# A fused attention and token-MLP kernel: one score tile moved from the end to the head of 39 stretches

## The chip, the core and the metric

The kernel runs on one core of a Trainium2 chip. A core has a matrix engine (TensorE, in the profile PE, with its weight loads as PEld), a vector engine (VectorE, DVE), a scalar engine (ScalarE, ACT), a general engine (GpSimd, POOL) and a queue that issues transfers (SyncE, SP). Each works through its own instructions in the written order and waits at semaphores for the others. Matrix products land in PSUM, which has eight banks of 128 x 512 fp32 numbers; VectorE and ScalarE read them from there.

The metric is the device time of one execution in microseconds (us); lower is better. Three runs of the kernel before gave 1671.33, 1671.52 and 1672.03 us, so the median is 1671.52 us.

## The reference

```python
x = A_x                                             # 2048 tokens x 640
g = _sigmoid((x * gate_w).sum(-1, keepdims=True))
a = _A_ref(x, A_wq, A_wk, A_wv, A_wo)               # attention: 32 heads of 20, one shared k and v
b = _B_ref(x, B_w1, B_b1, B_w2, B_b2)               # token MLP: W2 gelu(W1 layernorm(x)), over the tokens
return g * a + (1 - g) * b
```

Inside `_A_ref` the scores are `q @ k.T * 20 ** -0.5`, softmax runs over the 2048 keys, and the result goes through `wo`. Inside `_B_ref` the products are 2048 x 1728 and 1728 x 2048 for 640 channels. All is fp32: each large product is split into a high and a low part and done as three products of a faster type.

## The kernel before, in words

**Attention.** The work is cut into 32 groups (`NU`), each of four heads and 512 queries, and each group into 16 blocks of 128 keys: 512 units. Two kinds of score tiles are made, each of 128 x 512 numbers, one matmul and one PSUM bank:

- a *max tile* (`ms_next`, matmul at L479): queries on the rows. VectorE reduces it to a column of row maxima (`tensor_reduce`, L482). The maxima of a group must be known before its exponentials. There are 64 of them to a group, 2048 in all.
- an *exponent tile* (`s_next` and `qk`, L657): keys on the rows. ScalarE takes its exponential into SBUF (L660). Four belong to a unit.

When a unit is finished, `pv_mm` (L684) multiplies its four exponent tiles with v, in eight matmul records that run over four column parts of the array at a time.

**The banks.** From the start of the long middle part on (`ring`), max tiles and exponent tiles take turns on two pools of three banks each (`next_bank`). So whatever the kind, a tile gets the bank that the sixth tile before it had, and its matmul can start only when that tile has been reduced or exponentiated.

**Two row halves.** A score tile has only 60 or 62 rows of weights and takes one half of the 128 rows of the matrix array. In a stretch, one half (`b`) makes score tiles while the other half (`1 - b`) makes products of the MLP or of the projection, 320 columns wide (L929, L750 or L875, tile `g`). All products of an item, from both halves, add up in the one bank of `ps_g`. As the two halves must not write that bank at the same time, the first product of a stretch waits for a flag that VectorE writes after the last product of the stretch before (`signal`, L670). When an item is complete, its `done` has ScalarE copy the bank out (L758 for the second MLP product, L888 for the projection), and the next item's first product waits for that too.

**Stretches.** The list `ph` holds 326 stretches, and `main(k, vs)` writes out each. Even ones (call them *single*) finish one unit at their end, odd ones (*double*) two. The halves swap roles from stretch to stretch. A stretch has two lanes:

- the score lane, on half `b`: a string of `m` (max tile) and `s` (exponent tile), 11 letters, or 10 in one case;
- the product lane, on half `1 - b`: a string in which `F` is all products of the stretch, then the flag, then `done` if the item ends there, and `m` is a max tile on that half.

`merged` writes them into one order: at each step the lane goes that has used less time, with 0.232 us counted for a score tile and 0.147 us for a product. Two pairs of strings exist, by the number of products (`FEW` up to 15, `MANY` above), each for double and single:

```python
FEW = (("smsssmssmmm", "mFm"), ("smsmsmssms", "Fm"))
MANY = (("msmsmsssmsm", "Fm"), ("msmsmsssmsm", "Fm"))
```

**Which stretches there are.** 0 to 119: the first MLP product (20 items of six stretches, 16 products each). 120 to 249: the second MLP product for 13 blocks of tokens (26 items of five stretches with 16, 17, 16, 16 and 16 products). 250 to 285: the same for the last three blocks (six items of six stretches with 13 or 14 products). 286 to 325: the projection of ten blocks (20 items of two stretches with 15 products). After these follow `BLOCKS`, where no max tiles are left.

Between the lanes' work and the units, `main` also lets short pieces of older work go (`settle`: the transposes L700 and L712 and the reciprocal L705 that finish a group, on VectorE, at the end of double stretches), and reduces and stores row maxima (L493, L503).

Of the kernel before, what the change touches and what calls it, by code (L numbers as in the profile page):

```python
# [39 lines left out]
def mix_kernel(ctx: ExitStack, tc: tile.TileContext, A_x, A_wq, A_wk, A_wv, A_wo,  # L40
# [426 lines left out]
    def ms_next(b):  # L467
        k = given[b]
        if k >= 32 * NU:
            return None  # L470
        given[b] += 1
        n, r = divmod(k, 32)
        (kq, pr), qt = divmod(r // 4, 2), r % 4

        def step():
            if n not in mtiles:
                mtiles[n] = mpool.tile([P, 16, 4], F32, name="mp")
            ms = next_bank()
            nc.tensor.matmul(ms, qmax[n][64 * b:64 * b + 60, pr, qt * P:(qt + 1) * P],  # L479
                             kst[64 * b:64 * b + 60, kq * NB:(kq + 1) * NB], start=True, stop=True)  # L480
            c = (2 * b + pr) * 4 + qt
            nc.vector.tensor_reduce(mtiles[n][:, c, kq:kq + 1], ms, axis=AX.X, op=ALU.max)  # L482
            issued[b] += 1
            if min(issued) == 32 * n + 1:
                new_qmax(n + 1)

        return step

    def ms_done():
        n = len(row_max)  # L490
        if n < NU and min(issued) >= 32 * (n + 1):
            mm = mmpool.tile([P, 16], F32, name="mm")
            nc.vector.tensor_reduce(mm, mtiles.pop(n), axis=AX.X, op=ALU.max)  # L493
            mn = mmpool.tile([P, 2, 16], F32R, name="mn")
            nc.gpsimd.tensor_scalar(mm, mm, -1.0, None, op0=ALU.mult)
            nc.gpsimd.tensor_copy(mn[:, 0, :], mm)
            nc.gpsimd.tensor_sub(mn[:, 1, :], mm, f32(mn[:, 0, :]))
            row_max[n] = mn

    def store_max(n):  # L500
        mn = row_max[n]
        mt = mpool.tile([P, 32], F32, name="mt")
        nc.vector.transpose(mt, f32(mn).rearrange("p j c -> p (j c)"))  # L503
        nc.sync.dma_start(out=m_scr[n], in_=mt)

    def fetch_max(n):
        src = m_scr[n].rearrange("(i j b r) e -> j b r i e", j=2, b=2, r=8)
        for b in range(2):
            for j in range(2):
                rows = f32(qtiles[n][64 * b + 60 + j:64 * b + 61 + j])  # L510
                nc.sync.dma_start(out=rows.rearrange("o p (t i e) -> o (p t) i e", i=4, e=32), in_=src[j, b][None])
# [131 lines left out]
    def s_next(b):  # L643
        j = sc[b]
        if j >= 2 * len(units):
            return None
        sc[b] += 1
        return lambda: qk(j // 2, j % 2, b)
# [202 lines left out]
    def tail_take(h, n):  # L851
        out = []
        while len(out) < n and tail[h] and tail[h][0][0] in loaded:
            out.append(tail[h].pop(0)[1])
        return out
# [101 lines left out]
    def stretches(seq):  # L957
        return [(rows[1 - b], rest if b else [], done if b else []) for rows, rest, done in seq for b in range(2)]

    ph = stretches(seq)  # L960
    ph[0][1].append(lambda: twin_u(0))
    m = len(ph)
# [27 lines left out]
    def merged(lx, lf):  # L990
        lanes, at, out = (list(lx), list(lf)), [0.0, 0.0], []
        while lanes[0] or lanes[1]:
            k = 0 if lanes[0] and (not lanes[1] or at[0] <= at[1]) else 1
            us, f = lanes[k].pop(0)
            if f:
                out.append(f)
            at[k] += us
        return out
# [5 lines left out]
    def settle(wide=False):  # L1004
        for _ in range(2 if spare[0] else 1):
            if later and (wide or spare[0] or not later[0][0]):
                f = later.pop(0)[1]
                if f:
                    f()
        pop_chain()  # L1010
# [6 lines left out]
    def main(k, vs):  # L1017
        b = k % 2
        fs, rest, done = ph[k]
        fill = [(F_US, f) for f in fs] + [(0.0, f) for f in [signal] + done]  # L1020
        if not vs:
            lx = [(3 * X_US, ms_next(b)), (3 * X_US, ms_next(b)), (X_US, s_next(b)), (X_US, ms_next(b))]
            lx += [(X_US, s_next(b)) for _ in range(3)]
            lf = fill + [(X_US, s_next(1 - b))]
        else:
            sx, sf = (MANY if len(fs) > 15 else FEW)[len(vs) == 1]
            lx = [(X_US, (s_next if c == "s" else ms_next)(b)) for c in sx]
            lf = []
            for c in sf:
                lf += fill if c == "F" else [(X_US, (s_next if c == "s" else ms_next)(1 - b))]  # L1030
        order = merged(lx, lf)
        known, kept = set(row_max), set(sent)
        wide = len(vs) == 2
        parted = wide and units[vs[0]][1] == NS - 1
        for i, f in enumerate(order):
            if wide and i == (len(order) + 1) // 2:
                settle()
                if parted:
                    pv_mm(vs[0])
            f()  # L1040
        ms_done()
        spare[0] = len(row_max) == NU
        settle(wide and not parted)
        if vs:
            n, kb = units[vs[0]][0] + 1, units[vs[0]][1]
            if n in kept and n not in back_in:
                fetch_max(n)
                back_in.add(n)
        for f in rest:
            f()  # L1050
        if vs and kb > 4 and n in known and n not in sent and n < NU:
            store_max(n)
            sent.add(n)
        for v in vs[parted:]:
            pv_mm(v)
# [3 lines left out]
    for k in range(len(ph)):  # L1059
        n = 0 if k == 0 else 1 + k % 2  # L1060
        main(k, list(range(v, v + n)))
        v += n
        if k == len(ph) - 4:
            raw = last_wo()
        if k == len(ph) - 2:
            w_last = split_last(raw)
# [5 lines left out]
    for n in BLOCKS:  # L1072
# [4 lines left out]
        while any(sc[b] < ends[b] for b in range(2)):  # L1077
# [4 lines left out]
        fs = [tail_take(b, len(tail[b]) if n == left else  # L1082
                        max(0, round(((own[b] + len(tail[b]) * F_US) * n / left - len(lanes[b]) * X_US) / F_US)))
              for b in range(2)]
# [79 lines left out]
```

## Time and profile before

| | |
|---|---|
| median of three runs | 1671.52 us |
| the profiled execution's own time | 1671.47 us |
| its span | 1669.7 us |
| TensorE busy | 1661.0 us (99%) |
| VectorE busy | 1435.7 us (86%) |
| ScalarE busy | 1188.0 us (71%) |
| GpSimd busy | 606.3 us (36%) |
| max tiles reduced (L482) | 1514 + 534 |
| exponent tiles (L660) | 1512 + 536 |

The span is 1.8 us shorter than the profiled execution's time; that execution lies 0.05 us under the median. The granted clock of TensorE is 1.00 over the whole span. A matmul counts as busy from its issue to its modelled end, and matmuls of the two row halves overlap, so 99% says that TensorE nearly always had one under way, not that it ran at its peak. In the rows of a timeline, the first number is the start in us from the span's start, the second the time that the row covers; `x3` merges three instructions of one kind. Tile names `ms` and `s` are the two bank pools, not the two kinds of tile: the kind is told by the line, L479 for a max tile and L657 for an exponent tile.

### The profile page before, as it was taken

What the parts mean: (1) busy time and instruction counts of PE and PEld (TensorE: products, weight loads), DVE (VectorE), ACT (ScalarE), POOL (GpSimd) and SP (SyncE); (2) the same over time, 40 slices, a digit from 0 to 9 for tenths busy, and PEclk for the clock granted to TensorE, in tenths of its full rate; (3) what the DMA queues carried; (4) which work ended last, traced back from release to release, by engine and by line L of the source; (5) the groups of instructions that cost most, each with busy time, mean ns of one, the idle gap of its engine ahead of it and who ended that gap; (6) DMA issues with size and microseconds to landing.
All of it is one profiled execution on the core that took longest, in us unless ns stands there. A gap on an engine that the chain in (4) does not pass through costs nothing.

```text
span 1669.7 us, 38827 instructions
## 1 busy us (share of the span) xinstructions
PE 1661.0 (99%) x14865; PEld 1105.5 (66%) x14865; DVE 1435.7 (86%) x2732; ACT 1188.0 (71%) x2346; POOL 606.3 (36%) x759
## 2 busy tenths in 40 slices
PE   9999999999999999999999999999999999999998
PEld 7899666666666666666666666666666566666665
DVE  6689899999989999988888988988888998988933
ACT  4434777777777777777777777777777777777775
POOL 6578555455455554422232332122122220111210
PEclk9999999999999999999999999999999999999999
DMA  7665222222132232222222222212222121333611
GB/s 211 205 176 137 79 71 69 78 58 78 53 84 73 71 82 74 58 60 62 66 75 74 55 62 66 61 52 71 63 66 60 55 65 41 96 111 113 189 51 39
DMA packets 178305, 138.20 MB, mean 83 GB/s; under 512 B 33306, under 2 KB 144055, under 8 KB 178119
## 3 DMA queue, kind: packets, MB, share of 16 engines
q1 hardware_dynamic: 177830, 135.39, 28.9%
q8 instruction: 117, 1.92, 0.5%
q14 instruction: 70, 0.57, 0.1%
q10 hardware_dynamic: 288, 0.33, 0.1%
HBM read 102.36 MB, written 31.65 MB: 80 GB/s over the span
## 4 chain that ended last, share of the span: by engine, by line
PE 95%; issue 2%; DVE 1%; SPq 1%; ACT 0%; DMA 0%; POOL 0%; POOLq 0%; DVEq 0%; ACTq 0%
PE o L684 28%; PE ms L479 18%; PE s L657 13%; PE g L750 10%; PE g L929 7%; PE ms L657 5%; PE pp L298 4%; PE s L479 3%; PE pu L586 3%; PE g L875 2%; DVE mp L482 1%; PE ms L831 0%; ACT p L660 0%; PE pt L290 0%; SPq L195 0%
## 5 line engine op out<-in xcount | busy, mean ns | idle before, releaser
L482 DVE TENSOR_REDUCE mp<-ms 128x1 f32<-128x512 f32 x1514 | 967.2, 685 | 130.2 <-PE ms L479 102.7
L660 ACT ACTIVATE p<-s 128x512 f32<-128x512 f32 x1512 | 820.6, 606 | 299.4 <-PE s L657 280.2
L479 PE MATMUL ms<-kst,qmx 60*128 60x512 f32 x1514 | 646.5, 433 | 1.7 <-DVE mp L482 1.7
L657 PE MATMUL s<-qst,kst 62*128 62x512 f32 x1512 | 601.6, 403 | 0.0
L684 PE MATMUL o<-p,v_sb 128*32 128x512 f32 x4096 | 511.3, 601 | 0.0
L479 PEld LDWEIGHTS ms<-kst,qmx 60*128 60x128 f32 x1514 | 279.0, 184 | 244.9 <-ACT p L660 114.7
L482 DVE TENSOR_REDUCE mp<-s 128x1 f32<-128x512 f32 x534 | 355.6, 683 | 12.0 <-PE s L479 11.8
L660 ACT ACTIVATE p<-ms 128x512 f32<-128x512 f32 x536 | 305.1, 599 | 56.8 <-PE ms L657 50.2
L657 PEld LDWEIGHTS s<-qst,kst 62*128 62x128 f32 x1512 | 278.5, 186 | 55.2 <-DVE flag L670 31.0
L929 PE MATMUL g<-slot,wh 64*128 64x320 f32 x1280 | 297.5, 311 | 0.0
L129 POOL TENSOR_TENSOR wl<-wr,wh 128x512 fp32r<-128x512 f32 x176 | 228.6, 1300 | 43.8 <-PE g L750 17.3
L479 PE MATMUL s<-kst,qmx 60*128 60x512 f32 x534 | 230.8, 441 | 0.4 <-DVE yo L525 0.4
L684 PEld LDWEIGHTS o<-p,v_sb 128*32 128x32 f32 x4096 | 97.5, 108 | 185.3 <-issue 177.2
L657 PE MATMUL ms<-qst,kst 62*128 62x512 f32 x536 | 216.8, 405 | 0.0
L929 PEld LDWEIGHTS g<-slot,wh 64*128 64x128 f32 x1280 | 211.6, 184 | 2.0 <-issue 1.7
L750 PE MATMUL g<-slot,wh 64*128 64x320 f32 x864 | 202.1, 313 | 0.1
L750 PE MATMUL g<-u,wh 64*128 64x320 f32 x864 | 201.7, 312 | 0.0
L929 PE MATMUL g<-slot,wl 64*128 64x320 f32 x640 | 199.6, 312 | 0.0
L706 POOL TENSOR_TENSOR ot<-ot,rl 128x512 f32<-128x512 f32 x30 | 31.6, 1052 | 346.6 <-DVE rl L705 346.6
L128 POOL CAST wh<-wr 128x512 fp32r<-128x512 f32 x144 | 88.3, 613 | 188.0 <-PE g L750 81.5
L750 PEld LDWEIGHTS g<-slot,wh 64*128 64x128 f32 x864 | 143.5, 184 | 4.9 <-ACT yo L758 4.0
L750 PEld LDWEIGHTS g<-u,wh 64*128 64x128 f32 x864 | 143.5, 184 | 1.1 <-issue 1.1
(202 smaller groups left out, 2092.8 us busy)
## 6 DMA issues: line engine op xcount, KB each, us to landing
wr<-in_B_w_dram SPq DMA_DIRECT2D x152, 256.0 KB
qmx<-q_scr SPq DMA_DIRECT2D x192, 80.0 KB
qst<-q_scr SPq DMA_DIRECT2D x192, 80.0 KB
slot<-o_scr SPq DMA_DIRECT2D x20, 320.0 KB
y_scr<-yo SPq DMA_DIRECT2D x16, 320.0 KB
o_scr<-oh SPq DMA_DIRECT2D x124, 40.0 KB
o_scr<-ol SPq DMA_DIRECT2D x124, 40.0 KB
q_scr<-qh SPq DMA_DIRECT2D x19, 256.0 KB
```

Of the source, the lines that this page charges most:

```text
L128: nc.gpsimd.tensor_copy(wh, wr)
L129: nc.gpsimd.tensor_sub(wl, wr, f32(wh))
L298: nc.tensor.matmul(pp, w, t, start=first and n == 0, stop=not more and n == len(steps) - 1)
L479: nc.tensor.matmul(ms, qmax[n][64 * b:64 * b + 60, pr, qt * P:(qt + 1) * P], kst[64 * b:64 * b + 60, kq * NB:(kq + 1) * NB], start=True, s ...
L482: nc.vector.tensor_reduce(mtiles[n][:, c, kq:kq + 1], ms, axis=AX.X, op=ALU.max)
L586: nc.tensor.matmul(pu[r][:, :HD2], w[rows, c, :], h[rows, st, :], start=(st == 0 and k == 0), stop=(st == NS - 1 and k == 2))
L657: nc.tensor.matmul(s, kst[64 * b:64 * b + 62, kb * P:(kb + 1) * P], q[64 * b:64 * b + 62, pr, :], start=True, stop=True)
L660: nc.scalar.activation(p, s, AF.Exp, scale=SCALE)
L684: nc.tensor.matmul(o[32 * hh:32 * hh + 32, :], v_sb[:, kb, :], ptiles.pop((u, hh)), start=(kb == 0), stop=(kb == NS - 1), skip_group_check ...
L750: other_tile(half, nc.tensor.matmul(hold["p"][:, :HD2], w[r, fc % HS, :], u[d][r, fc, :], start=(hold["n"] == 1), stop=(hold["n"] == 6 * F ...
L875: other_tile(half, nc.tensor.matmul(hold["p"][:, :HD2], o[r, c, :], w[r, c, d * HD2:(d + 1) * HD2], start=(hold["n"] == 1), stop=(hold["n" ...
L929: other_tile(half, nc.tensor.matmul(hold["p"][:, :HD2], w[r, st % HS, :], h[d][r, st, :], start=(hold["n"] == 1), stop=(hold["n"] == 6 * NS)))
```

## The change

A condition is added after the strings are chosen. It holds where the stretch before ended an item (`ph[k - 1][2]`) and where either a double stretch has more than 15 products or a single one has at most 15. Then one `m` of the product lane's string goes to its head: `Fm` becomes `mF`.

```diff
             sx, sf = (MANY if len(fs) > 15 else FEW)[len(vs) == 1]
+            if k and ph[k - 1][2] and (len(vs) == 2) == (len(fs) > 15):
+                sf = "m" + sf.replace("m", "") + "m" * (sf.count("m") - 1)
             lx = [(X_US, (s_next if c == "s" else ms_next)(b)) for c in sx]
```

It holds for 39 stretches: 13 double ones with 16 products (125, 135, ... 245), six single ones with 13 (250, 256, ... 280), and 20 single ones with 15 (286, 288, ... 324). The first MLP product has none: behind its items come single stretches with 16 products. No instruction is added or taken away. In these stretches the order becomes, with `X` for a tile of the score lane by number and kind, `M` for the moved max tile, and `F` for a product:

```
16 products, double   before  X0m F F X1s F X2m F F X3s ... X9s F X10m flag M
                      after   X0m M X1s F F X2m F F X3s ... X9s F F X10m F flag
15 products, single   before  X0s F F X1m F F X2s F X3m ... F F X9s flag M
                      after   X0s M X1m F F X2s F F X3m ... F X9s F F flag
```

## The prediction

> **What bounds the kernel now.** I read the page first (busy shares, the chain that ended last), then who waited for ScalarE's copies of finished items, then timelines of single stretches, engine by engine.
>
> ```profile
> span 1669.7 us, 38827 instructions
> ...
> PE 1661.0 (99%) x14865; PEld 1105.5 (66%) x14865; DVE 1435.7 (86%) x2732; ACT 1188.0 (71%) x2346; POOL 606.3 (36%) x759
> ...
> PE 95%; issue 2%; DVE 1%; SPq 1%; ACT 0%; DMA 0%; POOL 0%; POOLq 0%; DVEq 0%; ACTq 0%
> ```
>
> TensorE's stream sets the end: the chain lies on it for 95%. So each stretch is worth what moves its first matmul on v (L684, behind which the next stretch begins). VectorE's 86% is the other number to watch.
>
> ```profile
> L758 ACT ACTIVATE yo<-g,b2g,og_half x32: 633/643/654, 710.6 to 1416.5; 128x320 f32<-128x320 f32 x32
> ...
>   PEld g L750: 4.0, 13
> ```
>
> Products waited 13 times for the copy of a finished item. Those are the 13 double stretches that the change touches. The first of them (stretch 125), TensorE, then ScalarE, then VectorE:
>
> ```profile
> 710.80 0.50 PE L479 MATMUL ms<-kst,qmx 60*128 60x512 f32 x1
> 711.27 0.41 PE L750 MATMUL g<-slot,wh 64*128 64x320 f32 x1
> 711.28 0.50 PE L657 MATMUL s<-qst,kst 62*128 62x512 f32 x1
> ...
> 711.62 0.39 PE L479 MATMUL ms<-kst,qmx 60*128 60x512 f32 x1
> ...
> 713.51 0.50 PE L479 MATMUL ms<-kst,qmx 60*128 60x512 f32 x1
> 713.57 0.30 PE L750 MATMUL g<-slot,wh 64*128 64x320 f32 x1
> 713.72 0.40 PE L479 MATMUL s<-kst,qmx 60*128 60x512 f32 x1
> 714.05 0.64 PE L684 MATMUL o<-p,v_sb 128*32 128x512 f32 x4
> ...
> 710.58 0.64 ACT L758 ACTIVATE yo<-g,b2g,og_half 128x320 f32<-128x320 f32 x1
> ...
> 711.33 3.46 DVE L482 TENSOR_REDUCE mp<-ms 128x1 f32<-128x512 f32 x5
> 714.72 0.69 DVE L482 TENSOR_REDUCE mp<-s 128x1 f32<-128x512 f32 x1
> ```
>
> X0 starts at 710.80. The first product waits until the copy ends (710.58 + 0.64 = 711.22) and starts at 711.27; X1, behind it in the queue, at 711.28. From X2 (711.62) to X10 (713.51) a score tile follows each (713.51 - 711.62)/8 = 0.236 us, of which I use 0.23. The 16 products take 2.30 us from first to last: 0.25 for the first step, then (2.30 - 0.25)/14 = 0.146 each. M starts at 713.72, the v matmuls at 714.05: 3.25 us from X0. There is a real wait to fill: the first product starts 0.47 us behind X0.
>
> **What the change does to banks.** Nothing is added; M, a max tile, goes from the end to behind X0. A tile takes the bank of the sixth tile before it, so the order decides who waits for whom. With M at the head, in a 16-product stretch X6 takes M's bank, X8 that of X2 and X10 that of X4: all reduced by VectorE, in the order X0, M, X2, X4. Before, X10 had X4's bank too, but VectorE had no M ahead of it. In a single stretch of 10 score tiles X6 now takes M's bank, X7 that of X1, X9 that of X3, behind reductions M, X1, X3.
>
> The profile already has a stretch with that head, unchanged by the edit: the double one with 15 products, X0 M X1 (`mFm`). Its X7, the ninth tile, takes the bank of X1, the third.
>
> ```profile
> 1456.09 0.50 PE L657 MATMUL s<-qst,kst 62*128 62x512 f32 x1
> 1456.09 0.49 PE L479 MATMUL ms<-kst,qmx 60*128 60x512 f32 x1
> 1456.43 0.39 PE L479 MATMUL s<-kst,qmx 60*128 60x512 f32 x1
> ...
> 1457.61 0.39 PE L657 MATMUL ms<-qst,kst 62*128 62x512 f32 x1
> ...
> 1458.00 0.49 PE L657 MATMUL s<-qst,kst 62*128 62x512 f32 x1
> ...
> 1456.66 0.69 DVE L482 TENSOR_REDUCE mp<-ms 128x1 f32<-128x512 f32 x1 [0.20 <-PE ms L479]
> 1457.26 0.68 DVE L482 TENSOR_REDUCE mp<-s 128x1 f32<-128x512 f32 x1
> ```
>
> X0 and M start together at +0.00, X1 at +0.34. M's reduction starts at +0.57, X1's at +1.17: one each 0.60 to 0.61 us, each over 0.69 us after its start. X1's ends at 1457.26 + 0.68 = 1457.94, and X7 starts at 1458.00, 0.39 behind X6 where 0.23 is the step: 0.16 us late, with a release of 0.06. That is the price of this head, measured where the head stands now.
>
> **Part 1: 13 double stretches.** Times after X0 (710.80). X0 and M at 0.00, X1 at 0.34, first product still at 0.47 (the copy), X2 about 0.63, then 0.23 each: X6 would be at 1.57. Reductions: X0 at 0.53 (711.33), M 1.14, X2 1.75, X4 2.36. M ends at 1.83, so X6 starts at 1.88, 0.31 late; products behind it wait too. X2's reduction ends at 2.43, X8 starts at 2.49. X4's ends at 3.04, so X10 starts at 3.10, where it started at 713.51 - 710.80 = 2.71. The last product goes with X10. The v matmuls start 0.33 behind the last score tile (714.05 - 713.72): 3.43 against 3.25, a loss of 0.18. Were VectorE never late, the last product would start at 2.77 as now, M gone from behind it, and the v matmuls at some 2.77 + 0.25 = 3.02 (0.33 less the 0.08 by which a product is shorter: 0.23 - 0.15): a gain of 0.23. I take the loss, since X6, X8 and X10 follow from rows of this very stretch: 13 x 0.18 = 2.3 us; the ends for the range are -3.0 and +2.3.
>
> **Part 2: single stretches.** One with 15 products (296) as it is:
>
> ```profile
> 1461.06 0.50 PE L657 MATMUL ms<-qst,kst 62*128 62x512 f32 x1
> 1461.06 0.57 PE L875 MATMUL g<-slot 64*128 64x320 f32 x2
> 1461.40 0.40 PE L479 MATMUL s<-kst,qmx 60*128 60x512 f32 x1
> ...
> 1463.08 0.45 PE L875 MATMUL g<-slot 64*128 64x320 f32 x2
> 1463.27 0.41 PE L657 MATMUL s<-qst,kst 62*128 62x512 f32 x1
> 1463.37 0.40 PE L479 MATMUL ms<-kst,qmx 60*128 60x512 f32 x1
> 1463.70 0.64 PE L684 MATMUL o<-p,v_sb 128*32 128x512 f32 x4
> ...
> 1461.83 1.89 DVE L482 TENSOR_REDUCE mp<-s 128x1 f32<-128x512 f32 x3 [0.57 <-PE s L479]
> ```
>
> The first product starts with X0: two v passes lie between the copy and this stretch, so there is no wait to fill. X9 starts at 2.21, M at 2.31, v at 2.64. VectorE idled 0.57 us before X1's reduction; that is what M at the head would use.
> After: X0 and M at 0.00, X1 and the first product at 0.34. M's reduction at 0.57, X1's at 1.18, X3's at 1.79. X7 starts when X1's ends, 1.18 + 0.69 + 0.06 = 1.93 instead of 1.75; X9 when X3's ends, 1.79 + 0.69 + 0.06 = 2.54 instead of 2.21. Two products follow X9 (2.54, 2.69), then v at 2.69 + 0.25 = 2.94: a loss of 0.30. With VectorE on time, the last product would stand at 0.34 + 2.16 = 2.50 (it takes 2.16 from the first to the last now) and v at 2.75: still 0.11 lost, because the head pushes all products back by 0.34 and the tail returns less. 20 x 0.30 = 6.0 us, ends 2.2 and 6.0.
> With 13 products the score lane is the longer, nothing follows X9:
>
> ```profile
> 1288.23 0.49 PE L657 MATMUL ms<-qst,kst 62*128 62x512 f32 x1
> ...
> 1290.43 0.48 PE L657 MATMUL ms<-qst,kst 62*128 62x512 f32 x1
> 1290.84 1.06 PE L684 MATMUL o<-p,v_sb 128*32 128x512 f32 x8
> ```
>
> X9 stands at 2.20, v at 2.61. After: X9 at 2.54, v 0.33 to 0.41 later: 2.87 to 2.95, on average 2.91, a loss of 0.30. Six of these: 1.8 us (end below: 0).
>
> **Part 3: pieces that lie ahead of M on VectorE.** At the end of a double stretch VectorE may get a transpose, or transpose and reciprocal; before, these ran in the 0.57 us of idle time.
>
> ```profile
> 1436.02 0.26 DVE L705 RECIPROCAL rl<-ot 128x16 f32<-128x16 f32 x1
> 1436.19 1.82 DVE L482 TENSOR_REDUCE mp<-s 128x1 f32<-128x512 f32 x3
> ...
> 1443.98 0.70 DVE L712 STREAM_TRANSPOSE on<-ot 128x512 f32<-128x512 f32 x1
> 1444.65 1.89 DVE L482 TENSOR_REDUCE mp<-s 128x1 f32<-128x512 f32 x3
> ```
>
> These stretches begin (first score tile, which the products start with) at 1435.27 and 1443.87; M's reduction would start at 0.92 and 0.78 instead of 0.57: 0.35 and 0.21 later, and X9 with it, 0.56 us for each group that ends. A group ends each 16 units, and two stretches finish three units. The 40 stretches from 286 on hold 60 units, 3.75 groups; of the 36 from 250 on, with 54 units or 3.4 groups, a third of the single ones is touched, 1.1 groups. 4.9 x 0.56 = 2.7 us (ends 0 and 2.7).
>
> **What moves with it at no cost.** The transfers of the next group's queries (SP) are issued by its first max tile; they go at most one stretch, some 3 us, earlier or stay, with two buffers for them. GpSimd's queue keeps its order. The flag is written after the last product either way, and the v matmuls (0.9 us for a unit) cover it. The stretch behind has one reduction less in VectorE's queue and the same banks in turn; its own waits stay.
>
> **Sum.** 2.3 + 6.0 + 1.8 + 2.7 = 12.8 us. The profiled execution took 1671.47 us, 0.05 under the median: 1684.3 us, 0.77% slower.
>
> [...]
>
> **Rivals.**
> *VectorE is never late.* Then the ends of parts 1 and 2 hold: -3.0 + 2.2 + 0 = -0.8 us, 1670.7 us. For it: VectorE is idle 14% of the span. Against: X7 at 1458.00.
> *The wait behind the copy is filled and that is all (faster).* M at the head works in the 0.47 us, and the single stretches lose nothing. Its price comes from a double stretch with 16 products behind no finished item (127):
>
> ```profile
> 719.95 0.50 PE L479 MATMUL ms<-kst,qmx 60*128 60x512 f32 x1
> ...
> 722.85 0.64 PE L684 MATMUL o<-p,v_sb 128*32 128x512 f32 x4
> ```
>
> It has v 2.90 behind X0, against 3.25: 0.35 x 13 = 4.6 us, 1666.9 us. It is faster than can be mistaken only if the 26 single stretches lose under (4.6 - 3.3)/26 = 0.05 us each, 3.3 us being 0.2% of the time. For it: the 13 waits are real. Against: a third of each single stretch's loss (0.11 of 0.30) needs no late bank at all.
> *The lateness is handed on.* If the double stretch behind, which has 0.16 us of lateness already, loses as much again, 26 x 0.16 = 4.2 us more: 1688.5 us. Against: VectorE is idle between the two.
>
> **How the numbers follow.** My forecast has 0.72, and 1676 to 1688 us as its own range (below, part 1 as a gain and no part 3: -3.0 + 6.0 + 1.8 = 4.8 us more than before; above, the lateness handed on); never late 0.10; filled 0.08; handed on 0.10. The predicted time is 1684.3 us. From 1672.0 to 1690.0 us the two low cases are left out, 0.18. Three runs agree within 0.7 us, and I take these 0.2% as what can be told from no change: faster is "filled" alone, 0.08; same is "never late", 0.10; slower is the rest, 0.82.
>
> **What the changed profile would show.** Right: in stretch 125 X6 and X10 late, each right behind the end of a reduction; in single stretches of 15 products X7 and X9 late and v at about 2.94 behind X0; weight loads of exponent tiles waiting for L482 more often; VectorE idle at the ends of these stretches instead of the heads. Wrong: v at 3.02 in the touched double ones or at 2.75 in the single ones. The forecast fails if reductions of two waiting tiles follow each other faster than 0.60 us, or if a stretch behind a touched one is shorter than now.

## The result

The changed kernel takes 1686.02 us (median of five runs, 1684.53 to 1686.65), against 1672.03 us (1671.33 to 1672.61) for the kernel before in the same runs: the ratio is 1.0082, with a 95% interval from 1.0069 to 1.0095. It is slower by 14.0 us. The forecast was 1684.3 us and slower.

From the page of the changed kernel (span, busy shares, and the chain that ended last by engine):

```profile
span 1684.2 us, 38873 instructions
...
PE 1673.2 (99%) x14865; PEld 1106.3 (66%) x14865; DVE 1434.8 (85%) x2732; ACT 1192.5 (71%) x2346; POOL 606.2 (36%) x759
...
PE 92%; DVE 3%; issue 3%; DMA 1%; SPq 1%; ACT 0%; POOL 0%; POOLq 0%; DVEq 0%; ACTq 0%
```

The work of each engine is what it was: the same counts of matmuls and of VectorE's instructions, and VectorE is busy 1 us less. But VectorE now makes 3% of the chain instead of 1%. Who waited for it is seen in the view of waits (engine, tile and line that waited, then the releaser; us in total, times, longest). Of the kernel before:

```profile
PEld s L657 <- DVE mp L482: 7.7, 34, 0.8
...
PEld ms L657 <- DVE mp L482: 1.7, 2, 0.8
```

and of the changed one:

```profile
PEld s L657 <- DVE mp L482: 11.6, 51, 0.8
PEld ms L657 <- DVE mp L482: 10.6, 45, 0.8
...
  PEld g L750: 2.6, 13
```

Weight loads of exponent tiles waited 96 times for a row maximum to leave its bank, 36 times before. The last line, from the view of ScalarE's copy at L758, is the wait that the moved tile stands in: the products' 13 waits went from 4.0 to 2.6 us. So the tile did stand in that wait, but more was lost behind it.

Stretch by stretch, from the first score tile (X0) of one to that of the next, summed over each kind, in the two profiled executions:

| stretches | count | change, us |
|---|---|---|
| touched: double, 16 products | 13 | +2.55 |
| touched: single, 13 products | 6 | +2.51 |
| touched: single, 15 products | 20 | +9.09 |
| the double ones behind touched single ones | 25 | -1.08 |
| all others from 121 to 324 | 140 | +0.02 |

Together this is 13.1 us. The spans differ by 14.5 us: in this execution of the changed kernel X0 of stretch 125, the first that the change touches, came 1.51 us later (712.31 against 710.80 us), though the edit changes nothing ahead of it; in the eight other traces X0 of this stretch lies between 710.36 and 710.93 us. That part isn't counted as the change's, and why it came isn't shown.

Of the 13 touched double stretches, twelve lost 0.17 to 0.28 us each, 2.78 in sum, and one (235) won 0.23. In that one the first of the two units ends a group, and its v matmuls run in the middle of the stretch: X6 starts 2.85 us behind X0, when M's reduction has been over since 1.83 us, so VectorE's queue can't make it late.

The same stretches of the changed kernel as were shown of before. Stretch 125, TensorE, then VectorE:

```profile
712.31 0.50 PE L479 MATMUL ms<-kst,qmx 60*128 60x512 f32 x1
712.31 0.50 PE L479 MATMUL s<-kst,qmx 60*128 60x512 f32 x1
712.64 0.39 PE L657 MATMUL ms<-qst,kst 62*128 62x512 f32 x1
712.78 0.41 PE L750 MATMUL g<-slot,wh 64*128 64x320 f32 x1
...
714.18 0.49 PE L657 MATMUL s<-qst,kst 62*128 62x512 f32 x1
...
714.78 0.50 PE L479 MATMUL s<-kst,qmx 60*128 60x512 f32 x1
...
715.38 0.50 PE L479 MATMUL s<-kst,qmx 60*128 60x512 f32 x1
...
715.81 0.64 PE L684 MATMUL o<-p,v_sb 128*32 128x512 f32 x4
...
712.84 0.69 DVE L482 TENSOR_REDUCE mp<-ms 128x1 f32<-128x512 f32 x1
713.45 3.16 DVE L482 TENSOR_REDUCE mp<-s 128x1 f32<-128x512 f32 x5
```

X0 and the moved tile M start together, and the first product still starts at 0.47 us behind them. VectorE then has five reductions without a break. X6 (714.18) starts 1.87 us behind X0, X8 (714.78) 2.47 and X10 (715.38) 3.07, each with the step of VectorE's reductions, 0.60 us, between them instead of 0.47. The v matmuls come at 3.50 us instead of 3.25.

Stretch 296, single with 15 products, TensorE, then VectorE:

```profile
1469.59 0.49 PE L657 MATMUL ms<-qst,kst 62*128 62x512 f32 x1
1469.59 0.50 PE L479 MATMUL s<-kst,qmx 60*128 60x512 f32 x1
...
1471.49 0.49 PE L657 MATMUL ms<-qst,kst 62*128 62x512 f32 x1
...
1472.09 0.49 PE L657 MATMUL ms<-qst,kst 62*128 62x512 f32 x1
1472.09 0.55 PE L875 MATMUL g<-slot 64*128 64x320 f32 x2
1472.57 0.64 PE L684 MATMUL o<-p,v_sb 128*32 128x512 f32 x4
...
1470.15 0.69 DVE L482 TENSOR_REDUCE mp<-s 128x1 f32<-128x512 f32 x1 [0.32 <-PE s L479]
1470.76 1.87 DVE L482 TENSOR_REDUCE mp<-ms 128x1 f32<-128x512 f32 x3
```

M's reduction starts at 0.56 us and those of X1, X3 and X5 follow without a break. X7 (1471.49) starts at 1.90, X9 (1472.09) at 2.50 with the last two products behind it, and v at 2.98 instead of 2.64.

### The profile page after: what moved, and what is told of

Its sections match the earlier page's. It is cut to its first block, busy times and chain, and to the rows that moved or that the text cites. A ratio compares the mean times of both kernels' runs of the same rounds, so it can differ in the third digit from the quotient of the medians.

```text
span 1684.2 us, 38873 instructions
## 1 busy us (share of the span) xinstructions
PE 1673.2 (99%) x14865; PEld 1106.3 (66%) x14865; DVE 1434.8 (85%) x2732; ACT 1192.5 (71%) x2346; POOL 606.2 (36%) x759
## 4 chain that ended last, share of the span: by engine, by line
PE 92%; DVE 3%; issue 3%; DMA 1%; SPq 1%; ACT 0%; POOL 0%; POOLq 0%; DVEq 0%; ACTq 0%
PE o L684 28%; PE ms L479 18%; PE s L657 13%; PE g L750 10%; PE g L929 7%; PE ms L657 6%; PE pp L298 3%; PE s L479 3%; PE pu L586 2%; PE g L875 2%; DVE mp L482 2%; PE ms L831 0%; DMA xa<-in_A_x_dram 0%; DMA q_scr<-ql 0%; ACT p L660 0%
## 5 line engine op out<-in xcount | busy, mean ns | idle before, releaser
L482 DVE TENSOR_REDUCE mp<-ms 128x1 f32<-128x512 f32 x1494 | 952.6, 685 | 148.4 <-PE ms L479 123.5
L660 ACT ACTIVATE p<-s 128x512 f32<-128x512 f32 x1492 | 810.6, 605 | 302.0 <-PE s L657 275.4
L479 PE MATMUL ms<-kst,qmx 60*128 60x512 f32 x1494 | 638.8, 433 | 2.6 <-DVE mp L482 2.6
L657 PE MATMUL s<-qst,kst 62*128 62x512 f32 x1492 | 594.1, 403 | 0.1
L479 PEld LDWEIGHTS ms<-kst,qmx 60*128 60x128 f32 x1494 | 275.4, 184 | 245.0 <-ACT p L660 113.6
L482 DVE TENSOR_REDUCE mp<-s 128x1 f32<-128x512 f32 x554 | 369.9, 683 | 9.3 <-PE s L479 7.6
L660 ACT ACTIVATE p<-ms 128x512 f32<-128x512 f32 x556 | 322.0, 601 | 61.9 <-PE s L479 31.0
L657 PEld LDWEIGHTS s<-qst,kst 62*128 62x128 f32 x1492 | 274.9, 186 | 61.3 <-ACT p L660 33.4
L479 PE MATMUL s<-kst,qmx 60*128 60x512 f32 x554 | 243.7, 449 | 0.4 <-DVE yo L525 0.4
L657 PE MATMUL ms<-qst,kst 62*128 62x512 f32 x556 | 230.5, 415 | 0.4
```

The costliest lines, as they stand in the source:

```text
L657: nc.tensor.matmul(s, kst[64 * b:64 * b + 62, kb * P:(kb + 1) * P], q[64 * b:64 * b + 62, pr, :], start=True, stop=True)
L660: nc.scalar.activation(p, s, AF.Exp, scale=SCALE)
```

## The experiments

The theory on record: a score tile takes the bank of the sixth tile before it, and with a max tile at the head these banks are freed by VectorE's queue, one each 0.60 us, too late. The rivals: the wait behind ScalarE's copy is what counts; VectorE is never late and the place at the head costs by itself or nothing; the lateness is handed on to the stretches behind.

**Only the double stretches.**

```diff
-            if k and ph[k - 1][2] and (len(vs) == 2) == (len(fs) > 15):
+            if k and ph[k - 1][2] and len(vs) == 2 and len(fs) > 15:
```

> The head only in the 13 double stretches with 16 products, the 26 single ones as before. Theory (a score tile at the head waits for a bank that VectorE frees late): v matmuls 3.43 to 3.50 us behind X0 in the 13 stretches instead of 3.26, so 13 x 0.2 = 2.2 to 3.1 us more than before (ratio 1.0013 to 1.0019), single stretches at 2.62 as before. Rival (the wait behind ScalarE's copy is filled): 3.0 to 4.6 us less than before (0.997 to 0.998).

Measured: ratio 1.0015 (1.0007 to 1.0024), 1674.29 us against 1671.67 us. The 13 stretches together got 2.56 us longer, all others by 0.3 us in sum. The wait behind the copy is real and the tile stands in it, but this half of the change alone is a loss.

**Only the single stretches.**

```diff
-            if k and ph[k - 1][2] and (len(vs) == 2) == (len(fs) > 15):
+            if k and ph[k - 1][2] and len(vs) == 1 and len(fs) <= 15:
```

> The head only in the 26 single stretches, the 13 double ones as before. Theory: 20 x 0.37 plus 6 x 0.33 plus some 0.2 us for each transpose that stands ahead of the moved tile, 10 to 12 us more than before (ratio 1.006 to 1.007); together with the run that has only the double ones it gives the whole of the change. Rival (lateness is handed on): the double stretches behind have v later than 3.12 us behind X0, and the sum is not that of the parts. Rival (single stretches lose nothing): ratio 1.000.

Measured: ratio 1.0059 (1.0045 to 1.0073), 1681.79 us. The touched stretches got 9.20 us (15 products) and 2.49 us (13 products) longer; the double ones behind them got 1.03 us shorter in sum, so lateness isn't handed on. The two halves add up: 1.0015 and 1.0059 make 1.0074, within the interval of the whole change.

**The moved tile with a short reduction.** VectorE reduces 64 of the moved tile's 512 columns.

```diff
-    def ms_next(b):
+    def ms_next(b, cols=NB):
...
-            nc.vector.tensor_reduce(mtiles[n][:, c, kq:kq + 1], ms, axis=AX.X, op=ALU.max)
+            nc.vector.tensor_reduce(mtiles[n][:, c, kq:kq + 1], ms[:, :cols], axis=AX.X, op=ALU.max)
...
-                lf += fill if c == "F" else [(X_US, (s_next if c == "s" else ms_next)(1 - b))]
+                lf += fill if c == "F" else [(X_US, ms_next(1 - b, 64 if touched else NB))]
```

> All of the change, but VectorE reduces only 64 of the 512 columns of the moved tile in the 39 stretches (the maxima of the other 448 columns are left out). Theory (VectorE's queue is what makes the banks late): with the moved tile's reduction some 0.45 us shorter the waits at the ninth and eleventh tile go; v at about 2.75 us behind X0 in the single stretches with 15 products (2.63 before, 2.99 with the full reduction), at 2.61 in those with 13, at about 3.03 in the double ones (3.26 before, 3.50 with the full reduction). Sum 20 x 0.12 - 13 x 0.23 = -0.6 us against before: ratio 0.999 to 1.001. Rival (the place of the matmul at the head costs by itself): ratio stays near 1.008.

Measured: ratio 0.9978 (0.9969 to 0.9987), 1668.20 us: 3.5 us faster than before, where the whole change is 14 us slower. The order of the matmuls is the changed kernel's. Stretch 296, TensorE, then VectorE:

```profile
1457.68 0.50 PE L657 MATMUL ms<-qst,kst 62*128 62x512 f32 x1
...
1459.44 0.40 PE L657 MATMUL ms<-qst,kst 62*128 62x512 f32 x1
...
1459.92 0.39 PE L657 MATMUL ms<-qst,kst 62*128 62x512 f32 x1
...
1460.31 0.64 PE L684 MATMUL o<-p,v_sb 128*32 128x512 f32 x4
...
1458.24 0.23 DVE L482 TENSOR_REDUCE mp<-s 128x1 f32<-128x64 f32 x1 [0.33 <-PE s L479]
1458.44 1.89 DVE L482 TENSOR_REDUCE mp<-ms 128x1 f32<-128x512 f32 x3
```

M's reduction covers 0.23 us instead of 0.69, and X1's follows it after 0.20 us instead of 0.61. X7 starts at 1.76 us and X9 at 2.24, within 0.03 us of the kernel before, and v at 2.63. The rows of this stretch show a loss of nothing at all, not the 0.11 us expected, and the gain is larger than the expected ratios (0.999 to 1.001) allow. The 13 double stretches won 2.94 us in sum, 0.23 each. Eight of the 20 single stretches with 15 products still lost 0.07 to 0.33 us each, 1.21 in sum: in these, one or two older pieces of VectorE's work (a transpose, or a transpose and a reciprocal) stand ahead of M, so VectorE is late there even with the short reduction.

**Control: the short reduction at the tail.** The kernel before, with the same tile of the same stretches left at the end and reduced over 64 columns.

```diff
+            touched = k and ph[k - 1][2] and (len(vs) == 2) == (len(fs) > 15)
...
-                lf += fill if c == "F" else [(X_US, (s_next if c == "s" else ms_next)(1 - b))]
+                lf += fill if c == "F" else [(X_US, ms_next(1 - b, 64 if touched else NB))]
```

> Control: the kernel before, with the same tile in the same 39 stretches still at the end, reduced over 64 of its 512 columns (the maxima of the other 448 columns are left out). All theories: VectorE idles behind that tile while the v matmuls run, so a shorter reduction is worth nothing there: ratio 0.999 to 1.000. If it is clearly below, the run with the short reduction at the head has to be read against this one.

Measured: ratio 1.0001 (0.9992 to 1.0009), 1671.68 us. The shorter work by itself is worth nothing; what matters is whether it stands ahead of the tiles whose banks are awaited.

**The moved tile reduced twice.** The opposite: the suspected cost is put in a second time.

```diff
-    def ms_next(b):
+    def ms_next(b, times=1):
...
-            nc.vector.tensor_reduce(mtiles[n][:, c, kq:kq + 1], ms, axis=AX.X, op=ALU.max)
+            for _ in range(times):
+                nc.vector.tensor_reduce(mtiles[n][:, c, kq:kq + 1], ms, axis=AX.X, op=ALU.max)
...
-                lf += fill if c == "F" else [(X_US, (s_next if c == "s" else ms_next)(1 - b))]
+                lf += fill if c == "F" else [(X_US, ms_next(1 - b, 2 if touched else 1))]
```

> All of the change, and the moved tile's reduction is made twice in the 39 stretches (same result). Theory (the reductions behind it in VectorE's queue decide): each touched stretch loses a further 0.60 us, one step between two reductions: v at about 3.6 us behind X0 in the single ones with 15 products, 4.1 in the double ones; 39 x 0.6 = 23 us more than the change, ratio to before near 1.022. Rival (only half of what VectorE does lies on the path): 10 us or less more than the change, ratio near 1.014.

Measured: ratio 1.0242 (1.0226 to 1.0258), 1711.80 us. Stretch 296 (the edit adds a line, so L483 is the reduction and L685 the v matmul):

```profile
1484.56 0.49 PE L658 MATMUL ms<-qst,kst 62*128 62x512 f32 x1
...
1487.20 0.50 PE L658 MATMUL ms<-qst,kst 62*128 62x512 f32 x1 [0.41 <-DVE mp L483]
...
1488.29 0.64 PE L685 MATMUL o<-p,v_sb 128*32 128x512 f32 x4
...
1485.13 1.42 DVE L483 TENSOR_REDUCE mp<-s 128x1 f32<-128x512 f32 x2 [0.33 <-PE s L479]
1486.46 1.88 DVE L483 TENSOR_REDUCE mp<-ms 128x1 f32<-128x512 f32 x3
```

X1's reduction starts at 1486.46, 1.90 us behind X0, against 1.17 in the changed kernel: 0.73 us later. Then v comes at 3.73 instead of 2.98, later by 0.75. In this stretch, what VectorE gets more, the stretch gets longer, one for one. Over all touched stretches it is 27.4 us more than with the change, 0.72 for each but one: 235 is 0.22 us shorter than before even with two reductions. The expected 0.60 us for a step was too small: the two reductions, which write the same column, cover 1.42 us, so with 0.69 us for the second it starts 0.73 behind the first.

**An exponent tile at the head instead.** In the 13 double stretches an exponent tile goes to the head, which ScalarE reads, and the single stretch behind gives it back.

```diff
+            if len(vs) == 2 and len(fs) > 15 and ph[k - 1][2]:
+                sx, sf = "msmsmsmsmsm", "sF"
+            elif k > 1 and len(vs) == 1 and len(fs) > 15 and ph[k - 2][2]:
+                sx, sf = "msmsmsmsmsm", "Fs"
```

> In the 13 double stretches with 16 products behind a finished item an exponent tile of the products' half (read by ScalarE) stands at the head instead of a max tile, and the score lane makes max tiles at every second place; the single stretch behind gives it back (an exponent tile at its end, one more max tile in its score lane). All else as before, the 26 single stretches too. Theory (the head slot is worth having where VectorE's queue does not grow at the head): no tile waits for a bank, v at 3.03 to 3.07 us behind X0 instead of 3.26, the single stretches behind as before; 13 x 0.2 = 2.5 to 3.0 us less than before, ratio 0.998 to 0.9985. Rival (any sixth tile behind the head is late, whoever reads it, or the lane of alternating max tiles makes VectorE late by itself): v at 3.26 or later, ratio 1.000 or above.

Measured: ratio 0.9989 (0.9981 to 0.9998), 1669.54 us against 1671.30 us. Stretch 125, and then the head of stretch 127 (TensorE, and the flag on VectorE):

```profile
710.40 0.50 PE L479 MATMUL ms<-kst,qmx 60*128 60x512 f32 x1
...
713.43 0.64 PE L684 MATMUL o<-p,v_sb 128*32 128x512 f32 x4
...
719.34 0.50 PE L479 MATMUL ms<-kst,qmx 60*128 60x512 f32 x1
719.58 0.41 PE L750 MATMUL g<-slot,wh 64*128 64x320 f32 x1
...
719.44 0.06 DVE L670 MEMSET flag<- 1x1 f32 x1
```

The 13 touched stretches won 3.02 us in sum: v at 3.03 us behind X0 instead of 3.25, with the head filled and no tile late. But 1.32 us came back in the double stretches two behind: the stretch that gives the tile back has six max tiles ahead of its flag, one more than before, the flag is written at 719.44, after the next X0, and the first product waits 0.24 us for it. The mechanism held, and the sum was smaller than expected by a cost that I hadn't counted.

**The string of the other double stretches.** As the run before, and in the 38 double stretches with 13 to 15 products, which have the head X0 M X1 in both kernels:

```diff
-    FEW = (("smsssmssmmm", "mFm"), ("smsmsmssms", "Fm"))
+    FEW = (("ssmsmsssmmm", "mFm"), ("smsmsmssms", "Fm"))
```

> The run with the exponent tile at the head, and in the 38 double stretches with 13 to 15 products, which have a max tile at the head in both kernels, the score lane's string is ssmsmsssmmm instead of smsssmssmmm: the tile whose bank the ninth one takes is then read by ScalarE at once, not by VectorE as the second in its queue. Theory: the ninth tile no longer waits (0.16 us now) and v comes about 2.99 to 3.05 us behind X0 instead of 3.12; 38 x 0.07 to 0.13 = 2.7 to 4.9 us less than the run with the exponent tile alone, ratio to before 0.995 to 0.997. Rival (the lateness only moves on to the twelfth tile): v stays at 3.12, ratio as in that run.

Measured: ratio 0.9978 (0.9969 to 0.9987), 1667.58 us, 1.96 us under the run before. Stretch 295, TensorE, then ScalarE:

```profile
1452.64 0.50 PE L657 MATMUL s<-qst,kst 62*128 62x512 f32 x1
...
1454.40 0.41 PE L657 MATMUL s<-qst,kst 62*128 62x512 f32 x1
...
1455.29 0.50 PE L479 MATMUL s<-kst,qmx 60*128 60x512 f32 x1
...
1455.72 1.06 PE L684 MATMUL o<-p,v_sb 128*32 128x512 f32 x8
...
1453.17 2.07 ACT L660 ACTIVATE p<-s 128x512 f32<-128x512 f32 x4 [0.57 <-PE ms L479]
```

X7 starts at 1.76 us: its 0.16 us of lateness is gone, as the theory says. But the last tile of the stretch, at 1455.29, starts 0.05 us after the fourth exponential ends (1453.17 + 2.07 = 1455.24), whose bank it takes, and v comes 0.43 us behind it: 3.08 us behind X0, where 3.12 was and 2.99 to 3.05 was expected. The expectation failed, in the sum too: 1.96 us, where 2.7 to 4.9 were expected. ScalarE set v in this stretch before as well. From the kernel before, TensorE's weight load for X10, then the fourth exponential, whose bank X10 takes:

```profile
1458.77 0.18 PEld L479 LDWEIGHTS ms<-kst,qmx 60*128 60x128 f32 x1
...
1458.12 0.60 ACT L660 ACTIVATE p<-ms 128x512 f32<-128x512 f32 x1
```

The load starts 0.05 us after that exponential ends (1458.12 + 0.60 = 1458.72), and v, at 1459.21, 0.44 us after the load. In 34 of the 37 stretches of this kind ahead of the last, v starts 0.48 to 0.49 us behind the end of the fourth exponential in the kernel before, and 0.47 to 0.49 in this one. So the 0.16 us at the ninth tile was a real wait, but v didn't depend on it there; v came 0.04 us sooner as the fourth exponential did (2.60 us behind X0 instead of 2.63). This kernel is faster than both kernels of the study, by 0.22% against the one before.

## Why the prediction was right

**Part 1 (13 double stretches, +2.3 us forecast): +2.55 measured,** as twelve losses and one gain, which the forecast hadn't. The step from bank to bank held to 0.03 us: X6, X8 and X10 at 1.88, 2.49 and 3.10 forecast, 1.87, 2.47 and 3.07 measured. Off was the end: with a score tile and a product starting together, v follows them by 0.43 us (715.81 - 715.38), not by 0.33.

**Part 2 (single stretches, 6.0 + 1.8 us): 9.09 and 2.51 measured, with part 3 in them.** X7 and X9 at 1.93 and 2.54 forecast, 1.90 and 2.50 measured. v stood at 2.98 instead of 2.94: the two products behind X9 cover 0.55 us (1472.09), of which the second's own time is 0.31, so the step between them is 0.24 us, where I counted 0.15.

**Part 3 (2.7 us).** Against the usual 0.37 us of loss, the stretches with a transpose and a reciprocal ahead of M lost 0.64 (290) and those with the other transpose 0.55 (292): 0.27 and 0.18 more, where 0.35 and 0.21 were forecast. Two (302 and 312) lost 0.68 and 0.80: there M's reduction starts 1.06 us behind X0 instead of 0.57, later than in the rows that the forecast went by. Without part 3, 20 x 0.37 + 6 x 0.33 = 9.4 us, so about 2.2 us of the 11.6 in the single stretches are its.

**The sum** was 12.8 us, the touched stretches alone made 14.15, and 1.08 came back in the double ones behind the single ones, which I had taken to stay. That was one of the forecast's own signs of being wrong, "if a stretch behind a touched one is shorter than now": 19 of the 25 are shorter by 0.03 to 0.06 us, and one, 311, by 0.32. In nearly all of these v follows ScalarE's fourth exponential, which ends sooner: in 295 2.60 us behind X0 instead of 2.63, in 311 2.60 instead of 2.92. Why it does isn't shown. The forecast of 1684.3 us is 1.7 us under the median. That the sum lies within 0.3 us of the 13.1 us of the stretches is partly chance: parts 1 and 2 came out larger by 0.25 and 1.6 us, part 3 smaller by 0.5, and the 1.08 us weren't forecast.

**What was wrong.** Two rivals were mispriced in the same step: "the head pushes all products back by 0.34 and the tail returns less", a loss of 0.11 us even with VectorE on time. With the short reduction at the head it was 0.00: the 2.16 us that I took from the first product to the last hold a slow first step, 0.26 us in stretch 296 of the kernel before (1461.06: two products cover 0.57 us, the second's own time is 0.31); with M at the head the first product comes behind X1, and the step in that run is 0.15 (1458.02: two products cover 0.45 us, of which 0.30 is the second's). So "VectorE is never late" was mispriced at 0.8 us less than before: the short reduction, with which VectorE is late in few stretches, gave 3.5 us less (2.9 by the stretches). The reason I gave against the rival "filled" (a loss that needs no late bank) was therefore no reason; the reason that held is the late bank, which the short and the double reduction show from both sides.

A reading was wrong too: the 0.16 us at X7 of the untouched stretch were called "the price of this head". They are the wait of one tile. In that stretch v hung on ScalarE's fourth exponential, and with the wait gone v came 0.04 us sooner, not 0.16. What carried over to the touched stretches was the step of VectorE's queue, 0.60 us from one reduction to the next, and there the last tiles did wait for it.

## What to carry to other kernels

Where tiles go round a ring of banks, the order of the tiles is also the order in which the readers must be done: before a tile is put into a gap, list for each tile behind it whose bank it takes and when that reader ends. A gap on one engine is worth filling with work whose reader has time just then; here the same gap of 0.47 us cost 2.6 us in sum with a tile for VectorE and gave 3.0 us with one for ScalarE (1.8 for the whole kernel). And look for a place in the same profile where the new order already stands: the untouched stretch showed how VectorE's queue makes the ninth tile late. But follow such a wait to the end of its stretch, since there something else set the time.

## What the runs showed of the hardware

Reductions of VectorE: in stretch 296 of the changed kernel two that write different columns start 0.61 us apart (1470.15, 1470.76); in the run with the double reduction the two that write the same column start 0.73 us apart there (1.42 us for both, less 0.69 for the second).

Products behind a wait: in stretch 296 of the changed kernel the two behind X9 cover 0.55 us, of which the second's own time is 0.31, so their step is 0.24 us. In stretch 125 the first product, which waited for the copy, starts at 712.78 and the second at 713.04: 0.26. The next two steps there are 0.14 and 0.15 us (713.18, 713.33). By an estimate from these numbers, each of these waits cost some 0.1 us more than its length.

Behind ScalarE: in stretch 295 of the kernel before, the weights of X10 were loaded 0.05 us after the end of the exponential that read its bank (1458.72, 1458.77), and the v matmuls started 0.44 us behind that load. In the run with the other string, the last tile of 295 started 0.05 us after such an end, and v 0.43 us behind it.
